# Keeping stored first-layer parts in idle on-chip columns instead of fetching them into one small buffer

## The chip, the cores and the metric

The kernel runs on one core of one Trainium2 chip. The metric is the device time of one execution in microseconds (us), taken as the median of several runs. One further execution was recorded by the hardware profiler; all rows below are from that one.

## The reference

Attention for 4 batches of 8 heads with 576 rows of 64 columns, in which each row keeps only its 32 largest scores, feeds a mixture of 8 experts in which every expert sees every row. The weight `P` of each row and expert comes from eight rounds of row and column normalisation.

```
scores = q @ k.T / sqrt(64);  keep the 32 largest of each row;  attn = softmax(kept)
x = (attn @ v) as rows [2304, 512]
P = exp(x @ w_gate - max), 8 rounds: P /= row sums; P /= column sums; P *= N / E
for e in range(8):
    h = max(x @ w1[e], 0)          # 512 -> 1024
    out += P[:, e] * (h @ w2[e])   # 1024 -> 512
```

All of it is in float32; each expert product is made of three matmuls on halves of the numbers (`wh`, `wl` of a weight, `xh`, `xl` of a row block, `hh`, `hl` of the hidden layer).

## The kernel before

The rows form nine blocks of 256 (`BLOCKS`): two for each batch and one of mixed remainders. Attention runs in five stages (`STAGES`); a stage yields the rows of its blocks. VectorE picks the 32 largest scores of each row (`topk`: MAX8 on L144 and MATCH_REPLACE8 on L147, 4 and 3 of them for 128 rows of a head), ScalarE makes the exponentials and copies, TensorE the products.

The experts work on blocks 0, 1, 2, 3 and 5 in turns (`visit`). Turn `v` runs expert `v % 8` for the blocks that are in at that time. Two blocks can be in at once: they sit in two seats, which are the column halves 0:256 and 256:512 of the same four tiles `xh`, `xl`, `hh` and `hl`. `BOARD = {0: 0, 1: 4, 2: 9, 3: 13, 5: 17}` says in which turn a block takes its seat. So in turns 0 to 3 block 0 is alone in the first seat (the lone turns, experts `ALONE = 0..3`), and the second seat's columns 256:512 of `hh` and `hl` hold nothing. Block 1 boards in turn 4, once stage two of attention is done; VectorE writes its `xl` on L89.

While the first attention stage still runs, the kernel does a first part of block 0's first layer, from those rows of `x` that are already there. `first_quarter` does a quarter for experts 4 to 7, `first_half` a half for experts 0 to 3. `part` copies each result from PSUM into a buffer `y` (ScalarE, L512) and stores it to a DRAM tile `p` (L514), 256 KB for each (expert, s), 32 in all. In turn `e`, `second_half` fetches it back into the tile `yp` (L546), which has a single buffer, makes the rest of the product on TensorE (`products`, L488), adds the stored part on VectorE (L552) and hands the sum to `store_hidden`: ScalarE writes `hh` (L556), VectorE writes `hl` (L557). Then the second layer reads `hh` and `hl` (L601). For each of the experts 0 to 7 `second_half` is called four times, `s` = 0 to 3. All these DMAs are issued from SyncE's queue (SP), in which the weight loads (L470 and L507, tile `wr`), the loads of q, k and v, and the stores of finished outputs (L611) also stand. Weights come as float32 in `wr`; ScalarE makes `wh` (L83), GpSimd makes `wl` (L86).

The order of the instructions on each engine is worked out when the program is built, by a planner that plays the program through with costs (`schedule_with_timeline_sim=True`); each engine then follows its list. `tc.high_priority(offset=2 * BIG)` puts the add and `store_hidden` ahead of other ready work. Ready weights of turn 0 are prepared by `first_half` (`ready`).

Of the kernel before, what the change touches and what calls it, by code (L numbers as in the profile page):

```python
# [7 lines left out]
F32 = mybir.dt.float32  # L8
# [38 lines left out]
ALONE, LATER = range(0, 4), range(4, 8)  # L47
# [4 lines left out]
def kernel(  # L52
# [11 lines left out]
    nc = tc.nc  # L64
# [14 lines left out]
    ap_ = actx.enter_context(tc.tile_pool(name="ap", bufs=2, side="right"))  # L79
# [332 lines left out]
    hh = hp_.tile([128, NFT, 512], F32R, name="hh")  # L412
    hl = hp_.tile([128, NFT, 512], F32R, name="hl")
# [66 lines left out]
    def products(ps, f0, seat, n, wh, wl, k0):  # L480
        nk = wh.shape[1]
        cs = slice(seat.c0, seat.c0 + n)
        for fo in range(512 // n):
            fs = slice((f0 + fo) * 128, (f0 + fo + 1) * 128)
            i = 0
            for kk in range(nk):
                for a, x in ((wh, seat.xh), (wh, seat.xl), (wl, seat.xh)):
                    nc.tensor.matmul(ps[:, fo, :], a[:, kk, fs], x[:, k0 + kk, cs],  # L488
                                     start=(i == 0), stop=(i == 3 * nk - 1))
                    i += 1  # L490
# [11 lines left out]
    PART = {}  # L502

    def half_weights(e, s2, half):
# [2 lines left out]
            nc.sync.dma_start(wr[:, r], w1[e, 2 * s2 + r, :, 2 * half:2 * half + 2, :])  # L507
        return wr

    def part(e, s, ps):  # L510
        y = op_.tile([128, 512], F32, name="y", bufs=YB)
        nc.scalar.activation(y, ps.rearrange("p a b -> p (a b)"), AF.Copy)  # L512
        PART[e, s] = dram.tile([128, 512], F32, name=f"p{e}_{s}")
        nc.sync.dma_start(PART[e, s], y)  # L514

    def first_quarter(x):
        for e in LATER:
            wr = wp.tile([128, 4, 256], F32, name="wr", bufs=WR)
            for s in range(4):
                nc.sync.dma_start(wr[:, s], w1[e, s, :, 0, :])  # L520
            for s in range(4):
                ps = ps1.tile([128, 2, 256], F32, name="p1")
                for fo in range(2):
                    nc.tensor.matmul(ps[:, fo, :], wr[:, s, fo * 128:(fo + 1) * 128], x[:, 0, :],  # L524
                                     start=True, stop=True)
                part(e, s, ps)

    def first_half(x):
        got = []
        for e in ALONE:  # L530
            for s2 in range(2):
                wr = half_weights(e, s2, 0)
                for r in range(2):
                    ps = ps1.tile([128, 2, 256], F32, name="p1")
                    for fo in range(2):
                        for kk in range(2):
                            nc.tensor.matmul(ps[:, fo, :], wr[:, r, kk, fo * 128:(fo + 1) * 128], x[:, kk, :],
                                             start=(kk == 0), stop=(kk == 1))
                    part(e, 2 * s2 + r, ps)
            if 0 < e < 4:  # L540
                got += [conversion(0, 2 * e - 2), conversion(0, 2 * e - 1)]
        return got

    def second_half(e, s, seat, wh, wl, k0):
        y = ap_.tile([128, 512], F32, name="yp", bufs=1)
        nc.sync.dma_start(y, PART[e, s])  # L546
        y = y.rearrange("p (a b) -> p a b", a=2)
        ps = ps1.tile([128, 2, 256], F32, name="p1")
        products(ps, 0, seat, 256, wh, wl, k0)
        ft = slice(2 * s, 2 * s + 2)  # L550
        with tc.high_priority(offset=2 * BIG):
            nc.vector.tensor_tensor(ps, ps, y, op=OP.add)  # L552
            store_hidden(seat, ft, slice(0, 256), ps)

    def store_hidden(seat, ft, cs, src):
        nc.scalar.activation(seat.hh[:, ft, cs], src, AF.Relu)  # L556
        nc.vector.scalar_tensor_tensor(seat.hl[:, ft, cs], src, 0.0, seat.hh[:, ft, cs].bitcast(F32),  # L557
                                       op0=OP.max, op1=OP.subtract)
# [8 lines left out]
    def visit(v, on):  # L567
# [10 lines left out]
        if groups:  # L578
            for s in range(4):
                wh, wl = convert(w1[e, s], [128, KD, 256])  # L580
                if on_first:
                    second_half(e, s, seats[0], wh[:, 1:4], wl[:, 1:4], 1)
                for seat, n in groups:
                    hidden(seat, n, s, wh, wl)
            ws = [convert(w2[e, s], [128, 2, 512]) for s in range(4)]
        else:
            got = ready.pop(v) if v in ready else [conversion(e, i) for i in range(6)]
            for s in range(4):
                wh, wl = got[s // 2]
                second_half(e, s, seats[0], wh[:, s % 2], wl[:, s % 2], 2)  # L590
            ws = got[2:]
# [289 lines left out]
```

## Time and profile before

| what | us |
|---|---|
| median of 3 runs | 1831.05 |
| lowest and highest of them | 1829.91, 1833.79 |
| the profiled execution's own time | 1833.39 |
| its span, first to last instruction | 1831.6 |

The profiled execution lies 2.34 us above the median; 1.79 us of its time lie outside its span. Its granted TensorE clock is 0.996 of full speed over the span. In the rows, "SPq" is SyncE's queue of DMA issues, "PEld" the weight loads of TensorE.

### The profile page before, as it was taken

The numbers are of one execution on the slowest core, as the hardware profiler recorded it, in microseconds if no ns is written. First come the engines' busy times: TensorE is split into PE (matmuls) and PEld (weight loads), VectorE is DVE, ScalarE is ACT, GpSimd is POOL, SyncE is SP. The second block draws the span as 40 slices with busy tenths as digits, with TensorE's granted clock in tenths as the row PEclk, the third lists the DMA queues.
The fourth block names the chain that finished last, engine by engine and source line by source line (L and its number), as shares of the span: only waits on it lengthen the run. The fifth ranks groups of instructions, "written<-read, shape, count | busy, mean of one in ns | idle before, by whom it ended". The sixth has DMA issues, their size and how long they took to land.

```text
span 1831.6 us, 26304 instructions
## 1 busy us (share of the span) xinstructions
PE 1785.6 (97%) x9385; PEld 1480.7 (81%) x9385; DVE 1207.9 (66%) x2232; ACT 1187.6 (65%) x1785; POOL 1068.3 (58%) x842
## 2 busy tenths in 40 slices
PE   4989999999999999999999999999999999999998
PEld 3777888888888878777787889888888888888887
DVE  8999998988888878878787141255555555533333
ACT  5888899999999888988897645533333333333331
POOL 4367856656766585556564688955544554554441
PEclk9999999999999999999999999999999999999999
DMA  4885877765767575656655356423333333211111
GB/s 136 264 260 174 255 198 178 207 191 160 199 174 179 143 223 170 168 152 164 172 152 142 90 174 217 161 98 109 114 117 104 104 107 114 90 58 63 53 35 46
DMA packets 227203, 270.77 MB, mean 148 GB/s; under 512 B 142464, under 2 KB 146688, under 8 KB 227072
## 3 DMA queue, kind: packets, MB, share of 16 engines
q1 hardware_dynamic: 226928, 268.83, 49.8%
q8 instruction: 73, 1.20, 0.3%
q14 instruction: 58, 0.48, 0.1%
q10 hardware_dynamic: 144, 0.26, 0.0%
HBM read 202.19 MB, written 34.60 MB: 129 GB/s over the span
## 4 chain that ended last, share of the span: by engine, by line
PE 83%; ACT 4%; POOL 4%; DVE 3%; DMA 3%; issue 3%; SPq 0%; ACTq 0%; POOLq 0%
PE p L601 20%; PE p L775 19%; PE p L488 18%; PE p L713 10%; PE pc L713 5%; PE pt L281 4%; DMA wr<-in_w_dram 2%; PE pb L713 2%; POOL wl L86 2%; PE sp L122 2%; PE sp L123 2%; DVE m L144 1%; DVE w L147 1%; PE p L524 1%; ACT wh L83 1%
## 5 line engine op out<-in xcount | busy, mean ns | idle before, releaser
L86 POOL TENSOR_TENSOR wl<-wr,wh 128x1024 fp32r<-128x1024 f32 x288 | 694.0, 2422 | 456.2 <-ACT wh L83 445.7
L83 ACT ACTIVATE wh<-wr 128x1024 fp32r<-128x1024 f32 x288 | 304.1, 1061 | 284.4 <-PE p L713 191.2
L144 DVE MAX8 m<-w 128x8 f32<-128x576 f32 x432 | 320.6, 753 | 5.8
L488 PE MATMUL p<-xh,wh 128*128 128x256 f32 (+1 forms) x832 | 274.7, 330 | 2.8 <-DVE hl L557 1.9
L488 PE MATMUL p<-xl,wh 128*128 128x256 f32 (+1 forms) x832 | 273.7, 329 | 0.1
L488 PE MATMUL p<-xh,wl 128*128 128x256 f32 (+1 forms) x832 | 273.0, 328 | 0.0
L601 PE MATMUL p<-wh,hh 128*128 128x512 f32 x640 | 250.2, 396 | 4.3 <-ACT hh L556 2.8
L601 PE MATMUL p<-wl,hh 128*128 128x512 f32 x640 | 249.6, 392 | 0.0
L601 PE MATMUL p<-wh,hl 128*128 128x512 f32 x640 | 241.3, 392 | 0.0
L147 DVE MATCH_REPLACE8 w<-m,w 128x576 f32<-128x576 f32 x288 | 213.7, 743 | 0.0
L775 PE MATMUL p<-wh,h2h 128*128 128x512 f32 x512 | 199.1, 389 | 0.6 <-DVE acc L618 0.6
L775 PE MATMUL p<-wl,h2h 128*128 128x512 f32 x512 | 199.2, 389 | 0.0
L775 PE MATMUL p<-wh,h2l 128*128 128x512 f32 x512 | 196.3, 389 | 0.0
L618 DVE SCALAR_TENSOR_TENSOR acc<-p,P,acc 128x512 f32<-128x512 f32 x120 | 89.5, 750 | 160.4 <-PE p L775 160.4
L557 DVE SCALAR_TENSOR_TENSOR hl<-p,hh 128x512 fp32r<-128x512 f32 x160 | 109.0, 682 | 106.5 <-ACT hh L556 105.5
L488 PEld LDWEIGHTS p<-xh,wh 128*128 128x128 f32 x832 | 157.6, 189 | 20.8 <-issue 2.1
L488 PEld LDWEIGHTS p<-xl,wh 128*128 128x128 f32 x832 | 157.7, 189 | 15.7 <-issue 0.9
L488 PEld LDWEIGHTS p<-xh,wl 128*128 128x128 f32 x832 | 157.6, 189 | 14.2 <-issue 0.5
L144 DVE MAX8 m<-s 128x8 f32<-128x576 f32 x144 | 108.4, 753 | 85.3 <-ACT s L134 84.8
L601 PEld LDWEIGHTS p<-wh,hh 128*128 128x128 f32 x640 | 120.1, 188 | 31.7 <-ACT hh L556 5.3
L601 PEld LDWEIGHTS p<-wl,hh 128*128 128x128 f32 x640 | 120.6, 188 | 23.4 <-issue 0.4
L601 PEld LDWEIGHTS p<-wh,hl 128*128 128x128 f32 x640 | 119.9, 188 | 23.6 <-DVE hl L557 0.2
(171 smaller groups left out, 3550.4 us busy)
## 6 DMA issues: line engine op xcount, KB each, us to landing
wr<-in_w_dram SPq DMA_DIRECT2D x248, 512.0 KB, 3.5
y<-y SPq DMA_DIRECT2D x160, 256.0 KB, 2.8
raw<-in_k_dram SPq DMA_DIRECT2D x48, 288.0 KB, 3.7
p<-y SPq DMA_DIRECT2D x32, 256.0 KB, 4.0
wr<-in_w_dram SPq DMA_DIRECT2D x32, 256.0 KB, 4.3
yp<-p SPq DMA_DIRECT2D x32, 256.0 KB, 3.3
raw<-in_q_dram SPq DMA_DIRECT2D x31, 256.0 KB, 3.5
values<-in_v_dram SPq DMA_DIRECT2D x24, 256.0 KB, 3.6
```

The lines of the kernel that those rows point to most:

```text
L83: nc.scalar.activation(dst, src, AF.Copy)
L86: nc.gpsimd.tensor_tensor(dst, src, hi.bitcast(F32), op=OP.subtract)
L122: nc.tensor.matmul(o, qc, kh[:, cs], start=(i == 0), stop=False)
L144: nc.vector.max(m8[:, u, r, :], ws[u] if r else units[u][0])
L147: nc.vector.match_replace(ws[u], m8[:, u, r, :], ws[u] if r else units[u][0], LOWEST)
L281: weighed = nc.tensor.matmul(av[r, 0:n], vr[:, o:o + 64], at[:, block, 0:n], start=(j == order[0]), stop=(j == order[-1]))
L488: nc.tensor.matmul(ps[:, fo, :], a[:, kk, fs], x[:, k0 + kk, cs], start=(i == 0), stop=(i == 3 * nk - 1))
L557: nc.vector.scalar_tensor_tensor(seat.hl[:, ft, cs], src, 0.0, seat.hh[:, ft, cs].bitcast(F32), op0=OP.max, op1=OP.subtract)
L601: nc.tensor.matmul(ps, a[:, ft, ts], m[:, ft % 2, :], start=(i == 0), stop=(i == 3 * NFT - 1))
L618: return nc.vector.scalar_tensor_tensor(ACC[t], y, g, ACC[t], op0=OP.mult, op1=OP.add)
L713: nc.tensor.matmul(ps, w[:, kk, :], x[:, kk, :], start=(fresh and i == 0), stop=(i == 5), skip_group_check=True)
L775: nc.tensor.matmul(ps, a[:, ft, ts], m[:, ft, :], start=(i == 0), stop=(i == 11))
```

## The change

The four stored parts of each of the experts 0 to 3 get a place in the second seat's unused columns: `place(e, s)` is rows `2s, 2s+1`, columns 256:512, of `hh` for even and `hl` for odd experts, read as float32. Experts 0 and 1: `part` copies `y` there at once by a DMA from one on-chip tile to the other, instead of the store to DRAM. Experts 2 and 3: `part` stores to DRAM as before; `second_half` of expert `e` issues, behind its own add and `store_hidden`, the fetch of expert `e + 2`'s part into the place that it has just read. In turns 0 to 3 `second_half` adds straight from the place. Experts 4 to 7 keep `yp`. Each place is two runs of 1 KB in a partition, where `y` and `yp` are one run of 2 KB.

```
+    def place(e, s):
+        return (hh, hl)[e % 2][:, 2 * s:2 * s + 2, 256:512].bitcast(F32)
+
     def part(e, s, ps):
         y = op_.tile([128, 512], F32, name="y", bufs=YB)
         nc.scalar.activation(y, ps.rearrange("p a b -> p (a b)"), AF.Copy)
+        if e in ALONE and e < 2:
+            nc.sync.dma_start(place(e, s), y.rearrange("p (a b) -> p a b", a=2))
+            return
         PART[e, s] = dram.tile([128, 512], F32, name=f"p{e}_{s}")
         nc.sync.dma_start(PART[e, s], y)
...
     def second_half(e, s, seat, wh, wl, k0):
-        y = ap_.tile([128, 512], F32, name="yp", bufs=1)
-        nc.sync.dma_start(y, PART[e, s])
-        y = y.rearrange("p (a b) -> p a b", a=2)
+        if e in ALONE:
+            y = place(e, s)
+        else:
+            y = ap_.tile([128, 512], F32, name="yp", bufs=1)
+            nc.sync.dma_start(y, PART[e, s])
+            y = y.rearrange("p (a b) -> p a b", a=2)
         ps = ps1.tile([128, 2, 256], F32, name="p1")
         products(ps, 0, seat, 256, wh, wl, k0)
         ft = slice(2 * s, 2 * s + 2)
         with tc.high_priority(offset=2 * BIG):
             nc.vector.tensor_tensor(ps, ps, y, op=OP.add)
             store_hidden(seat, ft, slice(0, 256), ps)
+        if e + 2 in ALONE:
+            nc.sync.dma_start(place(e + 2, s), PART[e + 2, s].rearrange("p (a b) -> p a b", a=2))
```

## Rows read from the trace of the kernel before

**Rows 1.** Busy time by stretch (columns named in its first line).

```profile
core 0: us, PE busy (x) PEld busy (x) DVE busy (x) ACT busy (x) POOL busy (x), PEclk, DMA share, GB/s
0.00:118.00 118.00, 88.57 (x435) 69.21 (x436) 102.59 (x218) 84.62 (x165) 53.59 (x65) 0.97 0.68 218
118.00:228.00 110.00, 104.63 (x650) 86.14 (x649) 108.05 (x217) 91.04 (x165) 87.54 (x70) 0.97 0.68 216
228.00:1070.00 842.00, 836.19 (x4788) 691.95 (x4786) 664.89 (x1315) 742.38 (x1079) 522.75 (x453) 1.00 0.62 170
1070.00:1831.60 761.60, 756.18 (x3518) 633.36 (x3516) 332.35 (x483) 269.56 (x378) 404.46 (x256) 1.00 0.32 103
```

**Rows 2.** The stored parts' buffer: instructions on tile yp, whole span.

```profile
L546 SPq DMA_DIRECT2D yp<-p x32: 319/327/536, 77.8 to 402.1; - x32
L552 DVE TENSOR_TENSOR p<-p,yp x32: 677/688/700, 123.6 to 413.0; 128x512 f32<-128x512 f32 x32
  DMA yp<-p: 1.3, 2
DMA to landing us min/median/max: 2.5/3.3/6.0
```

**Rows 3.** VectorE's groups in 118 to 228 us (busy, mean ns, idle before).

```profile
L144 DVE MAX8 m<-w 128x8 f32<-128x576 f32 x51 | 37.0, 746 | 0.0
L552 DVE TENSOR_TENSOR p<-p,yp 128x512 f32<-128x512 f32 x16 | 11.0, 688 | 0.4 <-DMA yp<-p 0.2
L89 DVE TENSOR_TENSOR xl<-xt,xh 128x256 fp32r<-128x256 f32 x5 | 5.9, 1183 | 1.8 <-ACT xh L83 1.8
```

**Rows 4.** Timelines of engines: expert 1, s = 1, near 152 us.

```profile
151.81 0.28 PE L488 MATMUL p<-xh,wl 128*128 128x256 f32 x1
152.14 0.33 SPq L546 DMA_DIRECT2D yp<-p  x1
153.80 1.41 PE L274 MATMUL pt<-idt,Et 128*128 128x128 f32 x6 [1.71 <-POOL Et L203]
155.72 0.70 DVE L552 TENSOR_TENSOR p<-p,yp 128x512 f32<-128x512 f32 x1
155.94 0.79 PE L601 MATMUL p<-wh,hh 128*128 128x512 f32 x1 [0.73 <-ACT hh L556]
```

**Rows 5.** TensorE's waits from 118 to 230 us (total, times, longest).

```profile
PE pt L274 <- POOL Et L203: 2.4, 2, 1.7
PE p L488 <- DVE hl L557: 1.0, 1, 1.0
PE p L488 <- ACT y L512: 0.9, 1, 0.9
PE p L601 <- ACT hh L556: 0.7, 1, 0.7
```

**Rows 6.** VectorE's timeline where block 1 boards.

```profile
226.22 0.43 DVE L89 TENSOR_TENSOR xl<-xt,xh 128x256 fp32r<-128x256 f32 x1 [0.17 <-ACT xh L83]
228.57 0.70 DVE L552 TENSOR_TENSOR p<-p,yp 128x512 f32<-128x512 f32 x1 [1.20 <-PE p L488]
```

**Rows 7.** Busy time by stretch, columns as in rows 1: clock and DMA share.

```profile
75.00:100.00 25.00, 22.92 (x118) 18.75 (x118) 21.99 (x50) 19.33 (x40) 11.52 (x15) 0.93 0.85 268
142.00:157.00 15.00, 12.49 (x73) 10.45 (x72) 14.95 (x32) 13.01 (x23) 10.88 (x10) 0.92 0.58 194
157.00:172.00 15.00, 15.00 (x85) 11.69 (x84) 15.00 (x32) 9.93 (x20) 9.23 (x10) 0.86 0.54 168
```

**Rows 8.** Waits of SyncE's queue and of ScalarE, 118 to 228/230 us.

```profile
SPq L546 <- DVE p L552: 10.9, 10, 2.5
SPq L546 <- DMA yp<-p: 6.4, 4, 2.7
ACT wh L83 <- DMA wr<-in_w_dram: 5.0, 4, 2.5
```

**Rows 9.** DMA issues (KB each, median us to landing).

```profile
p<-y SPq DMA_DIRECT2D x32, 256.0 KB, 4.0
yp<-p SPq DMA_DIRECT2D x32, 256.0 KB, 3.3
raw<-in_q_dram SPq DMA_DIRECT2D x31, 256.0 KB, 3.5
raw<-in_q_dram SPq DMA_DIRECT2D x16, 128.0 KB, 2.8
```

**Rows 10.** Timelines of ScalarE and VectorE near 85 us.

```profile
85.73 1.06 ACT L83 ACTIVATE wh<-wr 128x1024 fp32r<-128x1024 f32 x1 [3.65 <-DMA wr<-in_w_dram]
89.26 0.76 DVE L144 MAX8 m<-s 128x8 f32<-128x576 f32 x1 [3.01 <-ACT s L134]
```

## The prediction

> **What bounds the kernel now.** I read the busy time by stretch first [rows 1]. I cut the span where the work changes: before the lone turns, the lone turns (118 to 228 us), the attention stages beside full turns, and the expert work after attention. After 228 us TensorE is busy 836.19 of 842.00 us and then 756.18 of 761.60 us: there the end is set by the sum of TensorE's work, and a change can only win what TensorE idles (5.81 + 5.42 us by these rows) or make TensorE's backlog start earlier. In the lone turns it is VectorE that is full, 108.05 of 110.00 us, with TensorE at 104.63. So the question is: does anything in 118 to 228 us wait for the stored parts, and does the end of that stretch move?
>
> Second, the tile `yp` itself [rows 2]: 32 fetches, 2.5 to 6.0 us to landing, and VectorE sat idle for them twice in the whole span, 1.3 us together. In the lone turns it is 0.2 us [rows 3]. By the waits alone the fetches are hidden.
>
> Third, the timeline, because a wait that was filled with other work does not show as one [rows 4]. For expert 1, s = 1, the last matmul starts at 151.81 us and lasts 0.28, so the product stands at 152.09. The fetch could only be issued at 152.14, since the one buffer was still being read, and the add starts at 155.72. The add came 3.63 us later than the product allowed; VectorE did top-k work meanwhile. So the single buffer does hold up the chain add, `hh`, `hl`, second layer, without an engine showing it.
>
> Fourth, who misses that chain: TensorE's waits in the stretch [rows 5]. They add up to 5.0 us. Only two of the four can follow from a late add: 1.0 us for `hl` and 0.7 us for `hh`. The largest, 2.4 us, is for GpSimd's attention weights.
>
> Last, what ends the stretch [rows 6]. Block 1 boards with the `xl` written at 226.22 us, which comes out of VectorE's top-k of the second attention stage. However early the lone turns are done, the second seat is filled only then.
>
> **The change part by part.**
>
> *The fetches into `yp` for experts 0 to 3 go (16 of 32).* VectorE's idle time on them in the stretch is 0.2 us [rows 3]; that is gained in full. The adds stay: 16 at 688 ns, 11.0 us [rows 3], same shape and same engine; that the second operand lies in two runs instead of one is shown by no row, and I take nothing for it, since the add goes through PSUM in any case (bounds: 0, and for a loss the spread of the 32 adds, 16 x 23 ns = 0.4 us [rows 2]).
>
> *The adds can come earlier.* Each could by up to the 3.63 us of the one shown, where the buffer was late. What this gives is bounded by what waits for it: below 0, above the 1.7 us of TensorE's waits on `hl` and `hh` [rows 5] and, if the idle stretch around 152 us closes, the low clock that follows it. From 142 to 157 us the granted clock is 0.92 and from 157 to 172 us 0.86 [rows 7]: 15 x 0.08 + 15 x 0.14 = 3.3 us of full-speed work lost while TensorE partly ran at the lower of its two levels, 1.2 instead of 2.4 GHz, behind an idle time of 1.71 us and another of 0.73 us [rows 4]. The 1.71 us were ended by GpSimd, not by the add, so I don't expect them to close by themselves. Of 0 to 1.7 + 3.3 = 5.0 us I take 1.0, nearer to the waits that the add can reach.
>
> The Trainium skill (TensorE: Matmul & The Clock Gate, section "What's actually happening") says that the low clock is the default of an idle engine and that sustained work releases it. The trace agrees with the direction: 0.86 follows the idle time. By that rule closing the gap would give the whole 3.3 us, and the sum would be 5.3 instead of 2.0.
>
> *SyncE's queue.* In the stretch it stood 10.9 + 6.4 = 17.3 us before fetches into `yp`, 14 times [rows 8], with weight loads queued behind. Now 8 fetches are left there (expert 2 and 3's, behind the adds of expert 0 and 1), which wait for an add in the same way; the 8 in turns 2 and 3 are gone. So about half, 8.7 us, of queue time goes, and 8 issues. Who waits for what is queued behind: ScalarE, 5.0 us for weights in 4 waits [rows 8]; TensorE's list has no wait for a weight load [rows 5]. A mean queue wait is 17.3 / 14 = 1.2 us; taken off half of the 4 ScalarE waits that is 2.4 us of ScalarE, which is busy only 91.04 of 110.00 us [rows 1]. VectorE waits on ScalarE 1.8 us for `xh` [rows 3]. Bounds 0 and 1.8; I take 0.8.
>
> *The copies and the early fetches.* Eight stores to DRAM become on-chip copies, the same 256 KB each from the same `y`; eight loads vanish, and eight are made two turns ahead. A turn of the four is about 110 / 4 = 27.5 us [rows 1], so an early fetch has some 55 us where one needs 6.0 at most [rows 2]. Nothing of before copies 256 KB in runs of 1 KB. The nearest rows are the loads of q: 128 KB in rows of 1 KB land in 2.8 us, 256 KB in rows of 2 KB in 3.5 [rows 9]. So a 256 KB transfer in 1 KB runs should take from 2.8 to 2 x 2.8 = 5.6 us: 16 transfers between 0.5 us faster and 2.3 us slower than 3.3. Behind the 55 us of cover that costs 0. If the cover is gone for the eight copies, which run where the DMA engines are busy for 0.85 of the time [rows 7], up to 5.6 - 4.0 = 1.6 us each falls on what is queued behind them; that is the slow rival.
>
> *Sum.* 0.2 + 1.0 + 0.8 = 2.0 us less. Against the profiled execution's own 1833.39 us that is 1831.4; that execution lies 2.34 us above the median of the runs, so for the median 1831.05 - 2.0 = 1829.0 us. The lower and upper bounds of the terms give 0 to 0.2 + 5.0 + 1.8 = 7.0 us less without a reordering.
>
> One thing stands over all of it: the order on each engine is planned at build time. With other dependencies around 16 adds and 24 transfers the planner will place top-k, conversions and loads differently from about 70 us on. Such a reordering moves waits of 1 to 4 us about, like those in [rows 4, 10], and it can go either way.
>
> **The rivals.** What a measurement of this kernel can tell from no change is about 0.2%, 3.7 us.
>
> *Faster by more (chance 0.37).* The lone turns close up. For it: the buffer held back an add by 3.63 us [rows 4], and the turn's chain runs through four such adds. Against it: VectorE is full to 1.95 us in 110 [rows 1] and block 1 boards at 226.22 us [rows 6] whatever the lone turns do; TensorE could only pull forward the first seat's part of turn 4. All that can be won in the stretch is TensorE's idle 110.00 - 104.63 = 5.4 us and the 3.3 us of clock, 8.7 together. From 3.7 to 8.7 the middle is 6.2: 1824.9 us.
>
> *Slower (chance 0.23).* The on-chip copies, or the new order of the queue around them, bring weights later between 70 and 118 us. There ScalarE already stood 3.65 us before one weight load and VectorE, full from then on, stood 3.01 us behind ScalarE [rows 10]. Every further us that such a load is late goes through to VectorE, and from there to the boarding at 226 us, as nothing in between has room. It decides when the copies hold the next weight loads back by more than about 0.5 us each (8 x 0.5 = 4.0). With two more waits of 3.65 us the time would be 1831.05 + 7.3 = 1838.4; with the threshold just passed, 1835. Against it: a store that goes and a copy that comes are equal in bytes.
>
> The Trainium skill (Trace Analysis, section "DMA Optimizations") speaks for this rival: it says that transfers in pieces under 2 KB carry a notable overhead each. The row bears it out in part, with half the bytes in 0.8 of the time [rows 9].
>
> *Hidden anyway (chance 0.40), my forecast.* The adds move a little, VectorE's top-k still ends at about the same time, block 1 boards at about the same time, and 0 to 3.7 us are won. That the change doesn't do what it says, because the planner takes the two column halves of `hh` for one and orders a fetch behind all reads of `hh`, is in the slow cases: then L546-like waits on L601 would appear.
>
> **How the numbers follow.** The likeliest case gives 1829.0 us; its own range is 1827.4 to 1832. The fast case reaches down to 1831.05 - 8.7 = 1822.3, the slow one up to 1838.4. For 8 in 10 I leave out the outer part of each: from 1822 to 1837.5. Faster by over 0.2%: 0.37; within: 0.40; slower: 0.23, the three cases as they stand.
>
> **What would show it.** Right, if in the profile after VectorE's L552 of the lone turns starts within the time of one top-k instruction behind the last L488 of its product; if the last L89 of block 1's boarding stays within 2 us of 226.22; if VectorE is still busy about 108 of the 110 us; if no instruction waits for the early fetches. Wrong to the fast side, if the granted clock stays at 1.00 from 142 to 172 us and the boarding comes 4 us earlier or more. Wrong to the slow side, if ScalarE's waits for `wr` before 118 us grow beyond those of before, and the boarding comes later than 230 us.

## The result, and the profile after

The changed kernel takes 1853.68 us (median of 4 runs, 1850.67 to 1857.22), the kernel before 1830.54 beside it: 1.0119 of before, with a 95% interval of 1.0097 to 1.0141. It is slower by 1.2%, some 23 us, where 2 us less were forecast, and it lies above the range. The profiled execution took 1857.22 us.

First the page of the kernel after: its span, the busy time of the engines, the chain that ended last by engine, and the one TensorE group whose waits grew.

```profile
span 1855.3 us, 26300 instructions
...
PE 1793.6 (97%) x9385; PEld 1486.4 (80%) x9385; DVE 1209.1 (65%) x2232; ACT 1188.9 (64%) x1785; POOL 1069.9 (58%) x842
...
PE 70%; ACT 10%; DMA 6%; issue 5%; POOL 5%; DVE 4%; SPq 0%; POOLq 0%; ACTq 0%
...
L612 PE MATMUL p<-wh,hh 128*128 128x512 f32 x640 | 250.5, 396 | 11.1 <-ACT hh L567 11.0
```

The work is the same: 9385 matmuls, and 2232, 1785 and 842 instructions on the other engines, as on the page of before. TensorE's idle time is span less busy: 61.7 us, where before had 1831.6 - 1785.6 = 46.0. So 15.7 us of the 23.7 us longer span are idle time. The other 8.0 us are a busier TensorE; its granted clock over the span was lower (0.992, before 0.996), and 0.4% of the span is some 7 us.

By stretch, with the columns of [rows 1]:

```profile
0.00:118.00 118.00, 87.73 (x430) 68.46 (x431) 103.14 (x218) 85.89 (x166) 54.44 (x65) 0.97 0.67 218
118.00:228.00 110.00, 102.18 (x633) 84.71 (x631) 108.30 (x220) 90.67 (x161) 83.83 (x71) 0.97 0.60 190
228.00:1070.00 842.00, 823.76 (x4702) 680.23 (x4702) 658.68 (x1297) 734.39 (x1071) 512.36 (x447) 0.99 0.61 167
1070.00:1855.00 785.00, 779.91 (x3625) 653.03 (x3623) 338.96 (x499) 277.95 (x389) 419.23 (x262) 1.00 0.32 104
```

Against [rows 1], TensorE idles 2.5 us more in the lone turns, but 18.24 instead of 5.81 us in 228 to 1070 us, where nothing of the change is left to run: its last early fetch is issued at 167.1 us, as the next rows show. These are the instructions of the two new lines, the copies into the places (L517) and the early fetches (L564), each with its time from issue to landing. Column by column: engine, what it is, count, shortest, median and longest duration in ns, first and last start.

```profile
L517 SPq DMA_DIRECT2D hh<-y x4: 599/618/701, 74.9 to 81.8; - x4
L517 SPq DMA_DIRECT2D hl<-y x4: 606/606/606, 83.2 to 92.3; - x4
...
DMA to landing us min/median/max: 3.1/3.7/5.3
...
L564 SPq DMA_DIRECT2D hh<-p x4: 559/562/576, 123.5 to 140.8; - x4
L564 SPq DMA_DIRECT2D hl<-p x4: 524/543/559, 151.4 to 167.1; - x4
...
DMA to landing us min/median/max: 3.0/3.3/4.5
```

Under "who waited for it" both answers are empty. The copies and fetches are hidden, as forecast, and the places do their work: VectorE's adds in the lone turns, in its groups from 118 to 228 us, no longer wait for a fetch (0.2 us in [rows 3]).

```profile
L561 DVE TENSOR_TENSOR p<-p,hl 128x512 f32<-128x512 f32 x8 | 5.5, 682 | 0.1
L561 DVE TENSOR_TENSOR p<-p,hh 128x512 f32<-128x512 f32 x8 | 5.4, 680 | 0.0
```

The adds also start sooner behind their products. The one of [rows 4], for expert 1, s = 1, starts 0.43 us behind its product, which stands at 151.91 us:

```profile
152.34 0.68 DVE L561 TENSOR_TENSOR p<-p,hl 128x512 f32<-128x512 f32 x1
```

Over the 16 adds of the lone turns it is 0.87 us on average (0.04 to 2.20), where before has 2.57 (0.54 to 4.95). Each is counted from the end of the last matmul of its product on L488 to the start of the add.

What TensorE waits for from 118 to 1200 us (total, times, longest), after:

```profile
PE p L612 <- ACT hh L567: 11.0, 7, 3.4
PE pt L281 <- ACT at L171: 5.4, 2, 3.1
PE sp L122 <- ACT s L134: 3.7, 4, 1.3
PE pt L274 <- POOL Et L203: 3.2, 2, 2.7
PE p L488 <- DVE hl L568: 2.7, 4, 1.6
```

and in the same view of the kernel before, cut to those that answer:

```profile
PE p L601 <- ACT hh L556: 2.8, 3, 1.6
PE pt L274 <- POOL Et L203: 2.4, 2, 1.7
PE p L488 <- DVE hl L557: 1.9, 3, 1.0
PE sp L122 <- ACT s L134: 1.8, 2, 1.4
```

Three of the waits that grew are for ScalarE: 20.1 us after (`hh`, `at`, `s`), 4.6 before. Yet no wait is for the changed transfers. The boarding shows how an instruction can come to stand late. Three timelines of the kernel after, of TensorE, ScalarE and VectorE, cut to the instructions of block 1's last piece and those ahead of them:

```profile
227.55 0.65 PE L281 MATMUL pt<-at,values 128*64 128x256 f32 x2
...
226.72 2.11 ACT L164 ACTIVATE halves<-Et 128x2304 uint16<-128x2304 uint16 x1
...
229.26 2.41 ACT L171 ACTIVATE at<-turned 128x2304 uint16<-128x2304 uint16 x1
231.56 0.37 ACT L304 ACTIVATE xt<-pt 128x256 f32<-128x256 f32 x1
...
234.87 0.43 ACT L83 ACTIVATE xh<-xt 128x256 fp32r<-128x256 f32 x1
...
237.35 1.27 DVE L89 TENSOR_TENSOR xl<-xt,xh 128x256 fp32r<-128x256 f32 x1
```

The product stands at 228.20 us, but the lists have two attention copies of the next stage (2.11 and 2.41 us) and other work ahead, and `xl` is written at 237.35, not at 226.22 [rows 6]. The instructions are the same; their order is not. That gave the theory to be tested.

**Theory O:** the time comes from the order that the planner drew for the changed program. **Theory D:** it comes from the copies, the fetches or the places themselves.

### The profile page after: what moved, and what is told of

It reads as the page before. It is cut to its first block, busy times and chain, and to the rows that moved or that the text cites. A ratio compares the mean times of both kernels' runs of the same rounds, so it can differ in the third digit from the quotient of the medians.

```text
span 1855.3 us, 26300 instructions
## 1 busy us (share of the span) xinstructions
PE 1793.6 (97%) x9385; PEld 1486.4 (80%) x9385; DVE 1209.1 (65%) x2232; ACT 1188.9 (64%) x1785; POOL 1069.9 (58%) x842
## 4 chain that ended last, share of the span: by engine, by line
PE 70%; ACT 10%; DMA 6%; issue 5%; POOL 5%; DVE 4%; SPq 0%; POOLq 0%; ACTq 0%
PE p L786 19%; PE p L612 13%; PE p L488 13%; PE p L724 9%; PE pc L724 5%; POOL wl L86 3%; PE pt L281 3%; DMA wr<-in_w_dram 3%; PE pb L724 2%; ACT at L171 2%; ACT wh L83 2%; DVE m L144 2%; DVE w L147 1%; PE sp L122 1%; DMA turned<-halves 1%
## 5 line engine op out<-in xcount | busy, mean ns | idle before, releaser
L488 PE MATMUL p<-xh,wh 128*128 128x256 f32 (+1 forms) x832 | 276.9, 333 | 2.7 <-DVE hl L568 2.7
L488 PE MATMUL p<-xh,wl 128*128 128x256 f32 (+1 forms) x832 | 275.1, 331 | 0.3 <-POOL wl L86 0.3
L488 PE MATMUL p<-xl,wh 128*128 128x256 f32 (+1 forms) x832 | 275.3, 331 | 0.0
L488 PEld LDWEIGHTS p<-xh,wh 128*128 128x128 f32 x832 | 158.8, 191 | 21.2 <-DVE hl L568 3.6
L488 PEld LDWEIGHTS p<-xh,wl 128*128 128x128 f32 x832 | 158.8, 191 | 15.7 <-issue 0.8
L488 PEld LDWEIGHTS p<-xl,wh 128*128 128x128 f32 x832 | 159.0, 191 | 15.2 <-issue 0.4
```

## The experiments

Ratios are to the kernel before, run on the same chip, with 95% intervals.

**Orders exchanged.** In e1 the changed kernel's lists of TensorE, VectorE, ScalarE and GpSimd are put into the order of the kernel before, by dependencies within an engine that add no wait (SyncE's list is left to the planner). In e2 the kernel before gets the order of the changed one.

```
         tile_topk_attention__then__sinkhorn_moe_kernel(tc, *args)
+        pin(nc, tc)
...
+    for name, steps in json.loads(zlib.decompress(base64.b85decode(ORDER))).items():
+        at, before = 0, None
+        for step in steps:
+            at += step
+            i = of[name][at]
+            if before is not None:
+                tc.add_manual_dep(i, before.name, mybir.DependencyInfo(
+                    mybir.DependencyClass.NoSync, mybir.DependencyReason.DATA), reason="pinned")
+            before = i
```

> The changed kernel, with every instruction of TensorE, VectorE, ScalarE and GpSimd held in the order in which the kernel before has it (SyncE's queue is left to the planner). Theory O (the transfers and places cost nothing; the 23 us come from the order that the planner made of the changed program): 1825 to 1833 us. Theory D (the on-chip copies, the early fetches or the use of the hidden tiles' columns cost the time themselves): 1848 us or more, whatever the order.

> The kernel before, with the four engines held in the order of the changed kernel; all stored parts go through DRAM and the one buffer. Theory O: 1848 to 1862 us, as slow as the changed kernel or somewhat slower, since the buffer's waits fall where that order has no room for them. Theory D: 1828 to 1834 us.

e1: 1829.99 us, 0.9994 (0.9985 to 1.0003). e2: 1862.72 us, 1.0174 (1.0153 to 1.0194). With every transfer of the change but the old order nothing is lost; with nothing of the change but its order more is lost than by the change. e2 lies just above the range of theory O, and far from that of D. D falls, O stands.

The trace of e1 also shows the prediction's mechanism by itself. From the timelines of TensorE and VectorE, the last matmul for expert 1, s = 1, what VectorE did last before the add, the add, and the last `xl` of the boarding:

```profile
152.19 0.28 PE L488 MATMUL p<-xh,wl 128*128 128x256 f32 x1
...
155.31 0.73 DVE L147 MATCH_REPLACE8 w<-m,w 128x576 f32<-128x576 f32 x1
155.97 0.68 DVE L561 TENSOR_TENSOR p<-p,hl 128x512 f32<-128x512 f32 x1
...
225.32 0.43 DVE L89 TENSOR_TENSOR xl<-xt,xh 128x256 fp32r<-128x256 f32 x1 [0.41 <-ACT xh L83]
```

The add starts at 155.97, as at 155.72 in [rows 4], though nothing is fetched for it any more: it was its place in VectorE's list, behind top-k work, that kept it. The 16 adds start 3.27 us behind their products on average, no sooner than the 2.57 of before. The boarding is 0.90 us earlier than in [rows 6]. In e2 the single buffer `yp` meets the new order. Its instructions from 118 to 230 us, what their engine idled for and who waited for them (us, times):

```profile
  DMA yp<-p: 14.4, 5
...
  ACT hh L556: 13.6, 7
```

VectorE idles 14.4 us for fetches that cost 0.2 us in the old order [rows 3]. The same buffer is worth 1 to 2 us in one order and 9 in another (1862.72 against 1853.68).

**Halves of the change,** each with the order that the planner then draws:

```
e3:
-        if e in ALONE:
+        if e < 2:
...
-        if e + 2 in ALONE:
-            nc.sync.dma_start(place(e + 2, s), PART[e + 2, s].rearrange("p (a b) -> p a b", a=2))
e4:
-        if e in ALONE and e < 2:
-            nc.sync.dma_start(place(e, s), y.rearrange("p (a b) -> p a b", a=2))
-            return
...
-        if e in ALONE:
+        if e in (2, 3):
```

> Only the first half of the change: experts 0 and 1 are copied into the places, experts 2 and 3 keep DRAM and the one buffer; the planner makes its own order. Theory D: a share of the 23 us, and this run's loss and that of the fetches alone add up to 23 us. Theory O: a third order with a time of its own, anywhere from 1825 to 1860 us, and the two losses need not add up.

> Only the second half: experts 2 and 3 are fetched two turns ahead into the places, experts 0 and 1 keep DRAM and the one buffer; the planner makes its own order. Theory D: the rest of the 23 us that the copies alone don't cost. Theory O: again a time of its own from 1825 to 1860 us.

e3: 1852.07 us, 1.0109 (1.0092 to 1.0125). e4: 1857.41 us, 1.0141 (1.0125 to 1.0156). Either half alone costs as much as the whole, so the losses don't add up by parts. Each new program drew a new order: in the traces of e3 and e4, 4541 and 5328 of the 9385 matmuls stand at another place than before, 5261 in that of the changed kernel.

**An edit that changes no work.** In expert 3's first half the weight loads come in two pairs; the two loads of each pair are issued in the other order, in the kernel before (e5) and in the changed one (e6):

```
-        for r in range(2):
+        for r in ((1, 0) if e == 3 and not half else (0, 1)):
```

> The kernel before, in which only the two weight loads of each half of expert 3's first half are traced in the other order (the same transfers, the same work, no place). The planner makes another order of it, with 4342 of 8773 matmuls at another position. Theory O in its wide form (the order of the kernel before is a good one among many, and any new order costs about a per cent): 1840 to 1860 us. Narrow form (only the orders that the planner makes of the places are bad): 1828 to 1835 us. Theory D: 1828 to 1835 us.

> The changed kernel with the same two loads of expert 3 swapped: the planner makes an order that is nearer to that of the kernel before (1853 matmuls at another position, where the changed kernel has 4787). Theory O: the time goes with the order, so it lies apart from the changed kernel's 1853.7 us, between 1826 and 1850 us. Theory D: 1850 to 1857 us, since all transfers and places are those of the changed kernel.

e5: 1848.41 us, 1.0080 (1.0065 to 1.0096). e6: 1832.61 us, 1.0000 (0.9991 to 1.0009). The same line costs the kernel before some 15 us and takes the whole loss from the changed one. Against the lists of before, 4787 of 8773 matmuls that could be matched stand elsewhere in the changed kernel, 4342 in e5, 1853 in e6.

e6 has what the prediction hoped for, and in a planner's own order: its 16 adds start 1.06 us behind their products on average, and block 1 boards 5.2 us earlier than in [rows 6], as VectorE's timeline shows.

```profile
221.03 0.42 DVE L89 TENSOR_TENSOR xl<-xt,xh 128x256 fp32r<-128x256 f32 x1
```

Still it takes the time of the kernel before.

**Where the new order loses.** The changed kernel with one order up to 300 us and the other behind:

> The changed kernel, with the four engines held in the old order for all that the kernel before had begun by 300 us, and in the new order for the rest. By the start-to-start gaps of the matmuls in the two traces about 9 of the 24 us are lost before 300 us and 15 behind. If the loss sits in places of the order and adds up: 1843 to 1849 us. If it all follows from a late start of the full turns: 1829 to 1834 us.

> The changed kernel the other way round: the new order up to 300 us, the old one behind. If the loss adds up place by place: 1837 to 1843 us. If it all follows from the start of the full turns: 1850 us or more.

e7 (old, then new): 1852.23 us, 1.0102 (1.0082 to 1.0122). e8 (new, then old): 1837.48 us, 1.0031 (1.0017 to 1.0045). e8 lies in the range for a loss that adds up place by place; e7 lies above both of its ranges. By the ratios e8 has lost 7 us against e1 and e7 20, where the changed kernel has lost 23. Within the intervals the two parts add up, and most is lost behind 300 us. The 15 us behind 300 us that the expectation of e7 read from the two traces were too few.

**The hidden layer's writes ahead.** ScalarE's writes of `hh`, for which TensorE waits longest, are moved 1 to 4 places up its list: eight in the new order (e9), three in the old (e10).

```
ScalarE's list, two of the eight
-  L171 at, L83 qm, L83 wh, L567 hh, L567 hh
+  L567 hh, L567 hh, L171 at, L83 qm, L83 wh
```

> The changed kernel in its own order, with one difference: in ScalarE's list eight writes of the hidden layer, those that TensorE waited for near 208, 235, 248, 459, 491 and 962 us, are moved one to four places ahead, past weight conversions, transposed attention weights and output copies that stood before them. Added up, the product or the add was done 0.95 + 0.95 + 3.2 + 1.2 + 2 + 2.2 us, together some 10 us, before these writes began. If these waits in ScalarE's list are what the new order costs: 4 to 10 us less than the changed kernel, 1844 to 1850 us. If they only stand in front of other waits, as the rival has it: less than 2 us, 1852 to 1855 us.

> A version that might beat both: the changed kernel in the old order, with three writes of the hidden layer moved ahead in ScalarE's list in the same way (near 156, 417 and 1134 us, where TensorE waited 1.0, 1.6 and 1.1 us for them). If such waits are worth their length: 1826 to 1828 us, 2 to 4 us less than the changed kernel in the old order unmoved. If they move elsewhere: 1829 to 1832 us.

e9: 1853.70 us, 1.0123 (1.0108 to 1.0138): nothing is won, as the rival had it. TensorE's waits in e9, as in the view of after above:

```profile
PE p L612 <- ACT hh L567: 5.9, 3, 2.3
PE pt L281 <- ACT at L171: 5.8, 2, 3.3
...
PE p L612 <- ACT wh L83: 3.4, 1, 3.4
```

The wait for `hh` is halved, and others took its place. So the loss is not undone by moving these writes alone. e10: 1830.69 us, 0.9987 (0.9976 to 0.9998), next to nothing against e1's 0.9994.

**ScalarE's lateness.** If ScalarE as a whole runs late, work taken from it must help the new order more than the old. The copies into `at` are halved, which leaves out one of the two 16-bit planes, so the output is not the reference's; both orders are held:

```
-            nc.scalar.activation(at.bitcast(U16).rearrange("p g (c h) -> p g c h", h=2),
-                                 turned.rearrange("p h g c -> p g c h"), AF.Copy)
+            nc.scalar.activation(at, turned[:, 0], AF.Copy)
```

> The changed kernel in the order of the kernel before, with the 44 copies into at (L171, 2.40 us each on ScalarE) halved: each copies one of the two 16-bit planes as numbers, so the attention weights, and with them the output, are not the reference's. It takes some 44 x 1.2 = 53 us of work from ScalarE, all of it in the attention stages beside full turns, with every list of instructions as it was. Both theories expect the same here: TensorE's waits from 118 to 1200 us are only about 12 us in this order, few of them on ScalarE's attention copies, so 1826 to 1831 us. It is the base for the run beside it.

> The same halved copies in the order of the changed kernel. Theory S: the new order loses because ScalarE's list has its attention copies stand ahead of what TensorE needs (hh, s, at), so that ScalarE runs late; with 53 us of ScalarE's work gone most of the loss goes, and the difference to the run beside it falls from 22 to 24 us to under 10 us, 1840 us or less. Rival N: the loss is not ScalarE's lateness, but what the order lets each engine wait for (landings, other engines' results), so the difference stays at 17 us or more, 1845 us or more. Between 10 and 17 us both have a part.

e11: 1823.53 us, 0.9954 (0.9940 to 0.9967). e12: 1839.11 us, 1.0036 (1.0025 to 1.0048). e11 is faster than expected (1826 to 1831), so the old order gains from a lighter ScalarE too. The traces have 48 copies, not 44, of 2.40 us, and of 1.16 us when halved: 60 us of work went, not 53. The orders now differ by 15.6 us instead of 23.7: between the two theories. The stretches (columns as in [rows 1]) tell where. e1, after, e11 and e12, in this order, so that all four are the changed kernel:

```profile
0.00:300.00 300.00, 262.42 (x1590) 217.07 (x1591) 277.99 (x572) 245.43 (x427) 186.75 (x176) 0.98 0.66 204
300.00:1200.00 900.00, 893.02 (x5033) 742.17 (x5033) 625.74 (x1243) 737.83 (x1063) 587.05 (x468) 1.00 0.60 169
```

```profile
0.00:300.00 300.00, 257.90 (x1527) 212.55 (x1528) 278.23 (x569) 243.87 (x424) 178.57 (x171) 0.97 0.65 199
300.00:1200.00 900.00, 884.96 (x4992) 735.51 (x4991) 618.38 (x1232) 726.35 (x1047) 575.26 (x459) 0.99 0.60 168
```

```profile
0.00:300.00 300.00, 264.60 (x1602) 219.04 (x1602) 279.86 (x574) 242.02 (x432) 187.91 (x177) 0.99 0.66 206
300.00:1200.00 900.00, 898.98 (x5067) 749.85 (x5066) 630.12 (x1250) 689.64 (x1065) 587.27 (x468) 1.00 0.60 171
```

```profile
0.00:300.00 300.00, 256.28 (x1536) 210.80 (x1537) 279.20 (x572) 239.97 (x429) 180.95 (x174) 0.99 0.66 202
300.00:1200.00 900.00, 895.88 (x5064) 747.69 (x5063) 622.45 (x1242) 687.78 (x1059) 589.14 (x468) 1.00 0.60 170
```

From 300 to 1200 us the new order had 15.04 - 6.98 = 8.1 us more idle time on TensorE than the old; with short copies 4.12 - 1.02 = 3.1. So behind 300 us most of TensorE's extra idle time goes when ScalarE has less to do. Ahead of 300 us the difference did not shrink: 4.5 and 8.3. Only 5 of the 48 copies start there in the changed kernel, so these runs say little of what that part comes from.

**The boarding.** In the new order, only the three instructions of the late boarding are moved up (e13), and the same with short copies (e14):

```
ScalarE's list
-  L164 halves, L134 s, L171 at, L304 xt, ... L567 hh, L83 xh
+  L164 halves, L134 s, L304 xt, L83 xh, L171 at, ... L567 hh
VectorE's list
-  L561 add, ... L144 MAX8, L89 xl
+  L89 xl, L561 add, ... L144 MAX8
```

> The changed kernel in its own order, three instructions moved: block 1's last xt copy (L304) and xh (L83) directly ahead of the attention copy L171 on ScalarE, and xl (L89) ahead of the add on VectorE. The product stands at 228.2 us, so xl should be written near 231 instead of 237.35. Theory B (the boarding's place in the lists is what the new order loses ahead of 300 us): TensorE has the second seat's work 6 us earlier and 2 to 6 us are won against the changed kernel's own order, 1848 to 1852 us. Rival: the wait only moves, as with the hidden layers' writes moved ahead: 1852.5 to 1856 us.

> The same three moves and, as in e11 and e12, only one 16-bit plane copied into at, so the output is not the reference's. Theory B: the 15.6 us left between the orders with short copies fall by 2 to 6 us, 1833 to 1837 us. Rival: 1838 to 1841 us, as without the moves.

e13: 1852.07 us, 1.0113 (1.0094 to 1.0132). e14: 1837.27 us, 1.0026 (1.0014 to 1.0037). VectorE's timeline in e13:

```profile
226.74 1.76 DVE L89 TENSOR_TENSOR xl<-xt,xh 128x256 fp32r<-128x256 f32 x1
```

The boarding is 10.6 us earlier, and 1.6 to 1.8 us are won by the medians, which lies between the ranges of theory B and its rival and within what the intervals leave unsure. The boarding is at most a small part of the loss.

**A third of each copy on GpSimd,** with the whole computation, in the old order (e15) and in the new (e16):

```
+            au = at.bitcast(U16).rearrange("p g (c h) -> p g c h", h=2)
+            tu = turned.rearrange("p h g c -> p g c h")
+            nc.scalar.activation(au[:, 0:6], tu[:, 0:6], AF.Copy)
+            SPLIT.append(nc.gpsimd.tensor_copy(au[:, 6:9], tu[:, 6:9]).ins)
```

> The changed kernel in the order of the kernel before; of each copy into at (L171, 2.40 us, 48 of them) ScalarE does six of nine column groups and GpSimd three, put into its list where the copy started. That takes 48 x 0.8 = 38 us from ScalarE and gives GpSimd 48 pieces; nothing of before shows such a piece on GpSimd, the nearest are 1.44 us for 128x576 with two operands and 0.74 for 64x256, so between 0.8 and 1.9 us each. Halving the copies took 53 us from ScalarE and won 7 us in this order, so by theory S some 5 us are won here: 1824 to 1828 us, under both kernels. Rival: GpSimd's weights (wl, 2.4 us each, just in time for TensorE) come later by the pieces ahead of them and give it back: 1829 us or more.

> The same sharing in the order of the changed kernel, output as the reference's. Halved copies won 14.6 us here. Theory S, by the share 38/53: 10 us, 1841 to 1847 us, and the difference to the run beside it falls from 24 to about 18 us. Rival: GpSimd's pieces give it back, 1850 us or more, or the same few us are won as in the old order and the difference stays at 22 to 26 us.

e15: 1824.90 us, 0.9964 (0.9952 to 0.9977). e16: 1845.21 us, 1.0074 (1.0061 to 1.0087). The two kinds of piece in e15, by line:

```profile
L173 ACT ACTIVATE at<-turned x48: 1652/1664/1687, 228.9 to 1006.9; 128x1536 uint16<-128x1536 uint16 x48
...
L174 POOL COPY at<-turned x48: 904/918/992, 229.2 to 1005.6; 128x768 uint16<-128x768 uint16 x48
```

ScalarE is relieved of 48 x (2.40 - 1.66) = 35 us. By the ratios that is worth 0.0030 in the old order and 0.0045 in the new (5.5 and 8.2 us), so less work on ScalarE helps in both orders with the whole computation too. Both times lie in the ranges of theory S. That the new order gains more is not shown by this pair: the two gains differ by 0.0015, which is within their intervals, and the orders still differ by 20.3 us, between the 18 of the theory and the 22 of its rival. e15 is 0.4% faster than the kernel before, and so the fastest of the versions with the whole computation.

## Why the prediction was wrong

**The fetches, the adds, the queue, the copies (2.0 us less).** The runs don't contradict the sum, nor do they bear it out: e1 has all transfers of the change in the old order and stands 1.1 us under before by the ratio (2.7 less to 0.5 more), 1.6 by the medians, which is not told from nothing. Two of its readings fail. The late add in [rows 4] was not late for the fetch: with the fetch gone it stood where it was, 155.97 us. An engine that follows a list does not do other work "meanwhile"; what it did there stood ahead of the add in the list. The adds are earlier in orders that the planner drew anew, the changed kernel's and e6's, and e6 wins nothing by it. And the queue was not relieved by half: in e1 SyncE stood 16.4 us before the early fetches until an add was done, from 118 to 230 us, where the two rows for those into `yp` have 10.9 + 6.4 = 17.3 [rows 8]. ScalarE's waits for weights fell all the same, from 5.0 to 2.3 us, which is about the 2.4 that the prediction took off.

**The clock in that term.** From 142 to 172 us the granted clock was 1.00 in the profiled execution of e1, where before had 0.92 and 0.86 [rows 7], although the longest idle time, 1.71 us behind GpSimd's `Et` [rows 4], was still there. TensorE's timeline and the stretches of e1:

```profile
154.17 1.16 PE L274 MATMUL pt<-idt,Et 128*128 128x128 f32 x6 [1.71 <-POOL Et L203]
...
142.00:157.00 15.00, 12.24 (x75) 10.38 (x74) 15.00 (x31) 12.68 (x23) 10.88 (x9) 1.00 0.64 195
157.00:172.00 15.00, 15.00 (x95) 11.93 (x93) 15.00 (x30) 8.92 (x19) 9.60 (x10) 1.00 0.58 183
```

The Trainium skill (TensorE: Matmul & The Clock Gate, "What's actually happening") ties the clock to activity. These two executions don't show that: TensorE was busy for 12.24 us of the first stretch in e1 and for 12.49 before, and only e1 kept the full clock. Nor did the full clock show in the time: the profiled execution of e1 took 1833.30 us, that of before 1833.39. So the 3.3 us were the clock of one execution, and not a price of the late add.

**The step that failed** is the paragraph "One thing stands over all of it". It named what happened, a new order that moves waits of 1 to 4 us either way, and then the sum had no term for it, and the range none but the slow rival's two waits of 3.65 us. The single waits had about the size named: 3.4, 3.1, 2.7 us. But they did not balance: 15.7 us more idle time in all, 12.4 of it in 228 to 1070 us, which the change does not touch, and the prediction had priced effects in 70 to 230 us only. What orders cost is seen in the six that the planner drew itself, for programs in which TensorE's work is the same: 1831 (before), 1833 (e6), 1848 (e5), 1852 (e3), 1854 (after), 1857 us (e4). By these six a term of 0 to 26 us belonged in the range, with most of its weight on the slow side, as the order of before is the best of them. The prediction could not know the size; it put the term at next to nothing without a reason.

**The slow rival** gave the right sign for the wrong reason. Its mark was there, a boarding later than 230 us; its cause was not: ScalarE's waits for `wr` ahead of 118 us fell. Before, and then after:

```profile
ACT wh L83 <- DMA wr<-in_w_dram: 6.8, 3, 3.6
...
ACT wh L83 <- DMA wr<-in_w_dram: 3.9, 3, 1.6
```

So that the time went the way of this rival is luck. And e13 shows that the boarding, which the prediction took for the end of the stretch, can move by 10.6 us for a gain of under 2.

**The other marks.** VectorE was busy 108.30 us of the lone turns, and no one waited for early fetches: two marks of "hidden anyway" held while the time rose by 23 us. The mark of the adds held for about half of them, which start within the 0.75 us of one top-k instruction. That of the boarding failed (237.35 us). These were marks of the transfers and of the lone turns; none of them watched the order behind 228 us.

**What stays open:** what in the new order costs TensorE 4.5 to 8.3 us of idle time ahead of 300 us, the boarding aside; where the 15.6 us come from by which the orders still differ with short copies, beyond the 8.3 + 3.1 us of idle time; and why the planner's lists put ScalarE's copies where they run late.

## What to carry to other kernels

Where a planner writes the lists, an edit is two changes: its own effect and a new draw of the order, here some 1 us less (not told from nothing) and 23 us more. Compare the lists first, and time the edit with the old order held; an edit that changes no work shows how wide the draws lie. The bad draw showed here as more waits of TensorE for ScalarE (20.1 us where before had 4.6), and taking work from ScalarE (e15) helped in both orders.

## What the runs showed of the hardware

A transfer of 256 KB in runs of 1 KB held SyncE's queue for 0.52 to 0.70 us in the changed kernel, against 0.32 to 0.54 (0.33 in the middle) for a fetch in runs of 2 KB [rows 2]. It landed in 3.0 to 5.3 us (2.5 to 6.3 in e1), about as the 2.5 to 6.0 of those. In e15 a copy of 128x768 16-bit numbers took 0.92 us on GpSimd, 1.2 ns a column; ScalarE took 1.66 us for 128x1536, 1.1 ns a column. So GpSimd made this copy about as fast, and it could be shared.
